# Three raw weight slices and four squared tiles in the last block, and the experts' first loads on the slices' queue

## The chip, the core and the metric

The kernel runs on one core of one Trainium2 chip. The metric is the time of one execution on the device, in microseconds (us). A core has a tensor engine (PE; its weight loads are shown as PEld), a vector engine (DVE), a scalar engine (ACT), GpSimd (POOL) and a sync engine (SP). Every engine works through its own instructions in order. DMA transfers are issued as instructions of an engine (here SP, ACT and POOL) and are carried by the core's 16 DMA engines. Data lies in SBUF (128 partitions); matmuls write to PSUM.

## The reference

Three layers follow one another. Attention with a soft cap over 4 batches of 12 heads, 448 tokens each, gives `x` of 1792 x 768. A feed-forward layer takes `h = x @ w_in` (768 x 2048), `r = max(h, 0)`, `g = s * r*r + b`, `g @ w_out`. A mixture of 8 experts with 4 slots each follows: a softmax over the tokens gathers 32 slot inputs, each expert applies `w1` (768 x 1024), a rectifier and `w2` (1024 x 768), and a softmax over the slots spreads the result over the tokens:

```python
logits = x @ phi
slot_input = softmax(logits, over tokens).T @ x
for e in range(8):
    slot_out[e] = max(slot_input[e] @ w1[e], 0) @ w2[e]
return softmax(logits, over slots) @ slot_out
```

The weights come in as 64-bit numbers in `w_in` and `w_out` and as 32-bit numbers in `w1` and `w2`; the result is 1792 x 768 in 32 bits.

## The kernel before, in words

**Blocks.** The work goes batch by batch. `block(bi)` runs the feed-forward layer of batch `bi`, while the attention of batch `bi+1` is woven in between its steps. Block 3 is the last and has no attention beside it. After it comes `tail()`, the experts.

**One slice of a block (`hidden`, 16 per block, numbered `i` through all blocks).** `w_need(i+2)` (L358) asks for a raw slice `wr` of `w_in` (384 KB), which an earlier part has converted and stored in the DRAM scratch `wsc`. `w_split(i+1)` makes from each half of a raw slice a rounded part on ACT (the CAST, L370) and the remainder on DVE (L371); the two form one `ws` tile. 18 matmuls (L386) use the two `ws` tiles of slice `i`, 9 each. ACT then writes the rectified sum into an `r2` tile (L391) and squares it in place (L392).

**After a group of four slices (`post`).** The four `r2` tiles give the logits `L` (L415, 4 matmuls) and are turned by 4 transposes each (L401), which ACT copies to `g0` and `g1` (L403). After the fourth group, `chain` works out the softmax of the block: `lt`, `ln`, `et`, the product `pt` with `g` (L473) and `ct`. In block 3 this chain stands alone at the end, behind the last matmul of the layer. For block 2 it runs inside block 3.

**Buffers.** `turns(tag, i, kept, more, last, ...)` draws a tile from a pool `kp` that lives until the end of block 3 (`kept` buffers) or from a pool `tp` that is closed before block 3 (`more` buffers). From slice `last` on, only kept buffers are used. So `wr` has 2 + 1 buffers in the blocks 0 to 2 and 2 in block 3; `r2` has 5 + 4, and 5 in block 3; `ws` has 2 half-slice tiles in block 3. A load into a `wr` buffer waits until DVE has done the split that read it last. The order of every engine's instructions is set by the scheduler of the language when the program is built.

**The experts' weights (`prefetch`).** 27 tiles `wt` of 2 MB are loaded in halves of 1 MB (L521): three tiles of `w_out`, twelve of `w1`, twelve of `w2`. Seven slots are free as soon as block 2 ends; they are filled in block 3 with 14 halves, issued on ACT's queue, each placed behind the Square of a slice. Slots 7 and 8 lie where block 3 keeps its `x`, `wr`, `ws` and `r2`; slots 9 and 10 are `g0` and `g1`. Further tiles take the slots in turn. All 40 halves from there on are issued on SP's queue.

Of the kernel before, what the change touches and what calls it, by code (L numbers as in the profile page):

```python
# [7 lines left out]
F32 = mybir.dt.float32  # L8
F32R = mybir.dt.float32r
# [8 lines left out]
P = 128  # L18
B, H, S, D = 4, 12, 448, 64
# [4 lines left out]
KC = DM // P  # L24
FF = 2048
FC = FF // P
# [7 lines left out]
SCALE = 0.125  # L34
EPS = 1e-9
CAP_FAST = 40.0
GP = 3
STEPS = 8
DIRECT = 0
CASTS = NP  # L40
# [14 lines left out]
class Body:  # L55
# [228 lines left out]
    def conv_units(self):  # L284


        nc, io, c = self.nc, self.io, self.c
        cur = {}

        def place(fc):  # L290
            return self.turns("wr", fc, 2, 1, 3 * FC - 1, [P, KC * P], F32)

        def keep(fc, o):
            self.wr[fc] = o
            if self.f64:
                nc.sync.dma_start(self.wsc[fc], o)

        def across(fh, half):
            if half == 0:
                self.wide = True  # L300
                cur["o", fh] = self.cv.tile([P, KC * U], F32, tag="o", bufs=1, name="o")
            return cur["o", fh][:, half * CU:(half + 1) * CU]

        def proj(fh, half):
            if half == 0:
                return
            o = cur.pop(("o", fh)).rearrange("p (a b) -> p a b", b=U)
            self.later = [lambda: down(fh, o)]
            if self.f64:
                self.later += [lambda th=th: wturn(fh, th, o) for th in range(3)]  # L310
            self.later.insert(2, lambda: fold(fh))

        def down(fh, o):
            pp = self.bank("pp")
            for kc in reversed(range(KC)):
                j = kc % 4
                nc.tensor.matmul(pp[32 * j:32 * j + 32, :U], c["phi"][:, kc, :], o[:, kc, :], start=(kc + 4 >= KC), stop=(kc < 4))
            nc.scalar.copy(c["tmp"][:, S + U * (fh % 2):S + U * (fh % 2 + 1)], pp[:, :U])
            self.wide = self.f64

        def fold(fh):
            ps = c["tmp"][:, S + U * (fh % 2):S + U * (fh % 2 + 1)]
            pf = self.bank("pf")
            for j in range(2):
                nc.tensor.matmul(pf[:, 32 * j:32 * j + 32], ps[:, j * P:(j + 1) * P], c["fold"][:, :32], start=True, stop=True)
            nc.vector.tensor_copy(c["pw"][:, 2 * fh:2 * fh + 2, :], pf[:, :2 * NS].rearrange("p (a b) -> p a b", b=NS))
            self.nx = fh + 1
            if self.nx == FF // U:
                self.bias()

        def wturn(fh, th, o):
            tw = self.bank("tw")
            for j in range(2):
                for k in range(2):
                    nc.tensor.transpose(tw[:, (2 * j + k) * P:(2 * j + k + 1) * P], o[:, 2 * th + k, j * P:(j + 1) * P], c["idn"])
            n = o[:, 2 * th:2 * th + 2, :].rearrange("p a b -> p (a b)")
            nc.scalar.copy(n, tw)
            nc.sync.dma_start(self.osc[th][:, 2 * U * fh:2 * U * (fh + 1)], n)
            self.wide = th < 2

        units = []
        for fc in range(FC):
            units.append((io["w_in"][fc], lambda fc=fc: place(fc), lambda o, fc=fc: keep(fc, o), lambda fc=fc: self.nsplit + 3 > fc))
            for fh in range(FF // U):
                if XPOS[fh] == fc:
                    units += [(io["w_outT"][fh, h], lambda fh=fh, h=h: across(fh, h), lambda o, fh=fh, h=h: proj(fh, h), lambda h=h: h or not self.wide) for h in range(2)]
        return units

    def w_need(self, i):

        if i >= B * FC:
            return
        if i < FC:
            while i not in self.wr:
                next(self.conv)
        else:
            self.wr[i] = self.turns("wr", i, 2, 1, 3 * FC - 1, [P, KC * P], F32)
            self.nc.sync.dma_start(self.wr[i], self.wsc[i % FC] if self.f64 else self.io["w_in"][i % FC])  # L358

    def w_split(self, i):  # L360
# [13 lines left out]
    def hidden(self, bi):  # L374
        nc = self.nc
        x = self.xtile(bi)
        for fc in range(FC):
            i = bi * FC + fc
            self.w_split(i + 1)
            self.w_need(i + 2)  # L380
            ws = self.ws.pop(i)
            hp = self.psh.tile([P, 512], F32, tag="h", bufs=2, name="hp")
            k = 0
            for kc in range(KC):
                for w, s in ((0, 0), (0, 1), (1, 0)):
                    nc.tensor.matmul(hp[:, :S], ws[kc // 3][:, w, kc % 3, :], x[:, s, kc, :], start=(k == 0), stop=(k == 3 * KC - 1))  # L386
                    k += 1
                if kc in (1, 3):
                    yield
            r2 = self.turns("r2", i, 5, 4, 3 * FC - 5, [P, S], F32)  # L390
            nc.scalar.activation(r2, hp[:, :S], AF.Relu)  # L391
            self.mark = nc.scalar.activation(r2, r2, AF.Square).ins  # L392
            self.r2[i] = r2
            yield
# [118 lines left out]
    def prefetch(self, upto, behind=False):  # L513

        while self.nslot < min(upto, 54):
            k, h = divmod(self.nslot, 2)
            if h == 0:
                self.wt[k] = self.slot(k)
            src = (self.osc if self.f64 else self.io["w_out"])[k] if k < 3 else self.io["w1"][k - 3] if k < 15 else self.io["w2"][k - 15]
            with self.tc.issue_after(self.mark) if behind else nullcontext():  # L520
                (self.nc.scalar if behind else self.nc.sync).dma_start(self.wt[k][:, 2048 * h:2048 * (h + 1)],  # L521
                                                                       src[:, 2048 * h:2048 * (h + 1)])
            self.nslot += 1

    def run(self):
# [184 lines left out]
def tile_kernel(ctx: ExitStack, tc: tile.TileContext, io):  # L710
    nc = tc.nc
# [3 lines left out]
    def t(name, shape, dt=F32):  # L715
        c[name] = cp.tile(shape, dt, name="c_" + name)
        return c[name]
# [26 lines left out]
    nc.gpsimd.dma_start(c["hot"], io["hot"])  # L744
    for n in ("s", "b"):
        nc.gpsimd.dma_start(t(n, [P, 1]), io[n + "_"].partition_broadcast(P))
    nc.gpsimd.dma_start(t("selB", [P, GP, P], F32R), io["selB"].bitcast(F32R))
    nc.gpsimd.dma_start(c["phi"], io["phi"])
    t("pbrow", [P, NS])
    t("pb", [P, 1])  # L750
# [15 lines left out]
def layouts(inputs):  # L766
    import numpy as np
    cc = np.ascontiguousarray
    q, k, v = inputs["q"], inputs["k"], inputs["v"]
    a = {}  # L770
# [29 lines left out]
    for k in range(2):  # L800
        hot[:, k, k::2] = 1
    a["hot"] = hot
    selb = np.zeros((P, GP, P), np.float32)
    for j in range(GP):
        for i in range(2):
            k = 2 * j + i
            selb[32 * (k % 4) + k // 4, j, 64 * i:64 * i + 64] = 1
    a["selB"] = selb
    return a


# [14 lines left out]
```

## Time and profile before

| what | value |
|---|---|
| three runs | 693.52, 688.12, 691.66 us |
| median | 691.66 us |
| the profiled execution's own time | 690.2 us |
| its span, from the first to the last instruction | 688.3 us |
| PE busy | 621.2 us (90% of the span) |
| DMA, mean over the span | 199 GB/s |

The profile is of one execution, so what is read from it is set against that execution's 690.2 us. Its times are counted from the start of the span. Busy shares say little by themselves, since stages with different limits follow one another; they are read stage by stage, and in each stage the wait that ends last.

### The profile page before, as it was taken

To read this page: it belongs to the slowest core of one execution; us is meant where nothing else is said; L and a number is where in the kernel's file an instruction comes from. 1 tells how busy PE (TensorE), PEld (TensorE's weight loads), DVE (VectorE), ACT (ScalarE), POOL (GpSimd) and SP (SyncE) were. 2 spreads that over 40 slices of the span, in tenths; PEclk is the share of its full clock that TensorE was granted. 3 is DMA by queue.
4 is the path that set the end of the run, shared out by engine and by line. 5 is a ranking of instruction groups with operands and counts; after the bars stand their busy time and mean duration, and the time that the engine had idled before them with its cause. 6 is when DMAs were issued, how large, how long until landed. Compare 5 with 4: busy or idle time off the path is not lost.

```text
span 688.3 us, 10613 instructions
## 1 busy us (share of the span) xinstructions
PE 621.2 (90%) x4222; PEld 396.5 (58%) x4222; DVE 386.2 (56%) x574; ACT 413.7 (60%) x688; POOL 4.6 (1%) x12
## 2 busy tenths in 40 slices
PE   3968999999999999999999999999998987987662
PEld 2323566655566566566666666667877862445552
DVE  5999998998785674744546566455331223111211
ACT  4959788977886877578767777775543551010101
POOL 2000000000000000000000000000000000000000
PEclk9979999999999999999999999999999996999997
DMA  7534468677585633122222222102867848999997
GB/s 238 192 96 143 151 239 294 219 257 265 179 283 183 211 104 119 43 94 87 65 82 86 73 88 78 50 24 62 323 206 282 307 152 359 414 418 418 418 407 237
DMA packets 45642, 136.77 MB, mean 199 GB/s; under 512 B 4352, under 2 KB 23184, under 8 KB 38672
## 3 DMA queue, kind: packets, MB, share of 16 engines
q1 hardware_dynamic: 43136, 120.60, 49.4%
q10 hardware_dynamic: 2016, 14.68, 6.0%
q8 instruction: 35, 0.57, 0.4%
q0 software_dynamic: 432, 0.72, 0.3%
q14 instruction: 23, 0.19, 0.1%
HBM read 117.90 MB, written 18.09 MB: 198 GB/s over the span
## 4 chain that ended last, share of the span: by engine, by line
PE 54%; DMA 21%; DVE 12%; ACT 7%; issue 2%; SPq 0%; ACTq 0%; DVEq 0%
PE hp L386 25%; DMA wt<-in_w_dram 10%; PE U L173 8%; PE sc L113 6%; PE tp L401 4%; DMA wr<-wsc 3%; DMA raw<-in_w_outT_dram 3%; PE pt L473 2%; PE Sm L170 2%; DMA raw<-in_w_in_dram 2%; DVE es L158 2%; DVE rec L177 2%; DMA out_dram<-wt 2%; PE L L415 2%; ACT e L149 1%
## 5 line engine op out<-in xcount | busy, mean ns | idle before, releaser
L386 PE MATMUL hp<-x,ws 128*128 128x448 f32 x1152 | 279.7, 382 | 2.3 <-ACT ws L370 2.2
L386 PEld LDWEIGHTS hp<-x,ws 128*128 128x128 f32 x1152 | 204.9, 189 | 57.0 <-issue 38.6
L371 DVE TENSOR_TENSOR ws<-wr,ws 128x384 fp32r<-128x384 f32 x128 | 70.2, 555 | 102.9 <-ACT ws L370 100.0
L116 ACT ACTIVATE e<-sc,c_tsc 112x896 f32<-112x896 f32 x96 | 96.2, 1010 | 22.4 <-PE sc L113 22.0
L173 PE MATMUL U<-e,v 112*64 112x448 f32 x384 | 88.5, 553 | 11.3 <-DVE u L179 7.0
L370 ACT CAST ws<-wr 128x384 fp32r<-128x384 f32 x128 | 65.0, 514 | 46.8 <-PE hp L386 38.4
L149 ACT ACTIVATE e<-e,c_acap 112x1792 f32<-112x1792 f32 x48 | 86.3, 1797 | 0.4
L177 DVE RECIPROCAL rec<-Sm 128x448 f32<-128x448 f32 x24 | 71.0, 2958 | 16.3 <-PE Sm L170 15.2
L173 PEld LDWEIGHTS U<-e,v 112*64 112x64 f32 x384 | 29.5, 139 | 58.1 <-issue 48.0
L158 DVE TENSOR_TENSOR es<-es,e 112x896 f32<-112x896 f32 x48 | 52.3, 1089 | 18.5 <-ACT e L149 18.2
L113 PE MATMUL sc<-qh,kh 64*112 64x448 f32 x192 | 46.1, 463 | 9.3 <-DVE kh L74 6.2
L403 ACT COPY g<-tp 112x256 f32<-112x256 f32 x128 | 41.8, 379 | 14.1 <-PE tp L401 14.0
L391 ACT ACTIVATE r<-hp 128x448 f32<-128x448 f32 x64 | 34.9, 545 | 25.6 <-PE hp L386 25.4
L113 PEld LDWEIGHTS sc<-qh,kh 64*112 64x112 f32 x192 | 17.8, 177 | 45.1 <-issue 20.9
L401 PE MATMUL tp<-c_cst,r 128*112 128x128 f32 x256 | 40.1, 277 | 2.0 <-ACT r L392 1.6
L113 PE MATMUL sc<-qh,kl 64*112 64x448 f32 x192 | 39.3, 384 | 0.4 <-DVE kl L75 0.4
L113 PE MATMUL sc<-ql,kh 64*112 64x448 f32 x192 | 39.6, 384 | 0.0
L695 ACT COPY wt<-op 128x512 f32<-128x512 f32 x12 | 7.0, 585 | 53.8 <-PE op L690 53.8
L392 ACT ACTIVATE r<-r 128x448 f32<-128x448 f32 x64 | 37.4, 585 | 0.2
L401 PEld LDWEIGHTS tp<-c_cst,r 128*112 128x112 f32 x256 | 30.0, 134 | 11.8 <-ACT r L392 2.7
L170 PE MATMUL Sm<-es,c_ones 113*64 113x448 f32 x96 | 27.0, 581 | 1.4 <-DVE es L158 1.4
L674 PE MATMUL so_ps<-wt,xt 128*32 128x128 f32 x384 | 13.9, 276 | 13.0 <-DMA wt<-in_w_dram 13.0
(140 smaller groups left out, 580.2 us busy)
## 6 DMA issues: line engine op xcount, KB each, us to landing
wt<-in_w_dram SPq DMA_DIRECT2D x40, 1024.0 KB, 19.9
wr<-wsc SPq DMA_DIRECT2D x48, 384.0 KB, 3.1
raw<-in_w_in_dram SPq DMA_DIRECT2D x16, 768.0 KB, 4.5
raw<-in_w_outT_dram SPq DMA_DIRECT2D x16, 768.0 KB, 5.7
wt<-in_w_dram ACTq DMA_DIRECT2D x8, 1024.0 KB, 6.7
wsc<-wr SPq DMA_DIRECT2D x16, 384.0 KB, 3.3
osc<-o SPq DMA_DIRECT2D x24, 256.0 KB, 3.4
wt<-osc ACTq DMA_DIRECT2D x6, 1024.0 KB, 6.4
```

What stands on the lines that cost most here:

```text
L113: nc.tensor.matmul(sc[:, i, :S], k[r, c * CP:(c + 1) * CP], q[r, :], start=(j == 0), stop=(j == 2))
L116: nc.scalar.activation(self.e[p][-1][:, :, c % 2, :], sc[:, :, :S], AF.Tanh, scale=self.c["tsc"][:CP])
L149: self.nc.scalar.activation(e, e, AF.Exp, scale=self.c["acap"][:CP])
L158: nc.vector.tensor_add(es, es, e[:, :, k, :])
L170: nc.tensor.matmul(Sm[64 * i:64 * i + 64, :S], c["ones"][:CP + 1, :64], self.es[:CP + 1, i, :], start=(p >= DIRECT), stop=True)
L173: nc.tensor.matmul(U[64 * i:64 * i + 64, :S], v[:, i, k * D:(k + 1) * D], self.chunk(2 * p + i, k), start=(k == 0), stop=(k == NCH - 1))
L177: nc.vector.reciprocal(rec, Sm[:, :S])
L370: self.nc.scalar.copy(hi, u)
L371: self.nc.vector.tensor_sub(lo, u, hi.bitcast(F32))
L386: nc.tensor.matmul(hp[:, :S], ws[kc // 3][:, w, kc % 3, :], x[:, s, kc, :], start=(k == 0), stop=(k == 3 * KC - 1))
L401: self.nc.tensor.transpose(tp[:CP, q * P:(q + 1) * P], r2[:, q * CP:(q + 1) * CP], self.c["idn"])
L403: self.nc.scalar.copy(self.g[q][:CP, :, fc * P:(fc + 1) * P], tp[:CP, 2 * q * P:2 * (q + 1) * P].rearrange("p (a b) -> p a b", b=P))
```

## The change: what it does

The pools in block 3 hold three `wr` and four `r2` buffers in place of two and five. Over the blocks 0 to 2 both have as many as before (3 and 9). A third of the tile `selB` goes, and with it its load from DRAM (the tail writes the tile before it reads it). The 14 halves of block 3 are issued by SP.

```diff
@@ conv_units and w_need, twice
-            return self.turns("wr", fc, 2, 1, 3 * FC - 1, [P, KC * P], F32)
+            return self.turns("wr", fc, 3, 0, 3 * FC - 1, [P, KC * P], F32)
@@ hidden
-            r2 = self.turns("r2", i, 5, 4, 3 * FC - 5, [P, S], F32)
+            r2 = self.turns("r2", i, 4, 5, 3 * FC - 4, [P, S], F32)
@@ prefetch
             with self.tc.issue_after(self.mark) if behind else nullcontext():
-                (self.nc.scalar if behind else self.nc.sync).dma_start(self.wt[k][:, 2048 * h:2048 * (h + 1)],
-                                                                       src[:, 2048 * h:2048 * (h + 1)])
+                self.nc.sync.dma_start(self.wt[k][:, 2048 * h:2048 * (h + 1)], src[:, 2048 * h:2048 * (h + 1)])
@@ tile_kernel
-    nc.gpsimd.dma_start(t("selB", [P, GP, P], F32R), io["selB"].bitcast(F32R))
+    t("selB", [P, 2, P], F32R)
```

`GP` was 3. Lines of the changed kernel stand one lower up to the loads of the experts (L357 is L358 of before, L369 is L370, L520 is L521).

On SP, in block 3, before: only the loads of raw slices (`wsc_96` is the first slice of the block). In brackets stands what an instruction waits for; DVE is the split that frees the buffer, DMAHW an earlier transfer.

```order
L358 DMA wr<-wsc_96 128x768 [waits DMAHW7_49,DMAHW1_49,DVE_49]
L358 DMA wr<-wsc_97 128x768 [waits DMAHW0_49,DVE_49]
L358 DMA wr<-wsc_98 128x768 [waits DMAHW3_49,DMAHW1_49,DVE_49]
L358 DMA wr<-wsc_99 128x768 [waits DMAHW2_49,DVE_49]
L358 DMA wr<-wsc_100 128x768 [waits DMAHW3_49,DVE_49]
L358 DMA wr<-wsc_101 128x768 [waits DMAHW6_49,DVE_49]
```

On SP at the same place, with the change (`wsc_97` is the third slice of the block here; the names count one lower):

```order
L357 DMA wr<-wsc_97 128x768 [waits DMAHW3_49,DMAHW0_49,DVE_49]
L520 DMA wt<-osc_111 128x2048 [waits PE_49]
L520 DMA wt<-osc_111 128x2048
L357 DMA wr<-wsc_98 128x768 [waits DMAHW1_49,DVE_49]
L520 DMA wt<-osc_112 128x2048
L357 DMA wr<-wsc_99 128x768 [waits DMAHW2_49,DVE_49]
L520 DMA wt<-osc_112 128x2048
L357 DMA wr<-wsc_100 128x768 [waits DMAHW3_49,DVE_49]
L520 DMA wt<-osc_113 128x2048 [waits PE_49]
L357 DMA wr<-wsc_101 128x768 [waits DMAHW6_49,DMAHW4_49,DVE_49]
```

The halves now stand between the slices' loads, mostly one to one, and two in a row at three places: here, before `wsc_103` and before `wsc_108`. None of them waits for ACT, though the source still places them behind a Square.

On ACT, in the middle of block 3, before: two of the halves, with the CASTs of the next slices behind them.

```order
L370 CAST ws<-wr 128x384 [waits DMAHW4_49,DVE_49,PE_49]
L403 COPY g_4520<-tp 112x2x128
L521 DMA wt<-in_w_dram 128x2048 [waits DMAHW7_49]
L370 CAST ws<-wr 128x384 [waits DVE_49,PE_49]
L403 COPY g_4519<-tp 112x2x128
L403 COPY g_4520<-tp 112x2x128
L391 ACTIVATE r_4598<-hp 128x448
L370 CAST ws<-wr 128x384 [waits DMAHW6_49,DVE_49,PE_49]
L392 ACTIVATE r_4598<-r_4598 128x448 [waits Activation_49]
L521 DMA wt<-in_w_dram 128x2048 [waits DMAHW1_49]
```

On ACT at the same slices, with the change:

```order
L369 CAST ws<-wr 128x384 [waits DMAHW4_49,DVE_49,PE_49]
L402 COPY g_4518<-tp 112x2x128 [waits PE_49]
L402 COPY g_4519<-tp 112x2x128
L369 CAST ws<-wr 128x384 [waits DVE_49,PE_49]
L390 ACTIVATE r_4597<-hp 128x448
L391 ACTIVATE r_4597<-r_4597 128x448 [waits Activation_49]
L369 CAST ws<-wr 128x384 [waits DMAHW6_49,DVE_49,PE_49]
```

The halves are gone from ACT, and the Square stands ahead of the next slice's CAST, where it stood behind it.

On PE, inside block 3, the chain of block 2 (`et`, then the product `pt`), before:

```order
L386 MATMUL hp<-x_3396,ws 128x448 x18
L461 MATMUL et_ps<-c_cst,c_tmp 112x32 x4
L473 MATMUL pt<-g_3555,c_tmp 32x512 x8
L473 MATMUL pt<-g_3556,c_tmp 32x512 x8
L493 MATMUL ct_ps<-c_cst,c_tmp 128x112 x4
```

With the change:

```order
L385 MATMUL hp<-x_3395,ws 128x448 x9
L460 MATMUL et_ps<-c_cst,c_tmp 112x32 x4
L385 MATMUL hp<-x_3395,ws 128x448 x5
L472 MATMUL pt<-g_3554,c_tmp 32x512 x8
L472 MATMUL pt<-g_3555,c_tmp 32x512 x8
L385 MATMUL hp<-x_3395,ws 128x448 x10
L492 MATMUL ct_ps<-c_cst,c_tmp 128x112 x4
```

Matmuls of the layer now stand between `et` and `pt`. The blocks 0 to 2 and the tail keep their order on PE.

## Rows read from the trace of the kernel before

**Rows 1.** Windows by stage: block 3, its closing chain, the tail's loads, the end.

```profile
core 0: us, PE busy (x) PEld busy (x) DVE busy (x) ACT busy (x) POOL busy (x), PEclk, DMA share, GB/s
479.70:561.90 82.20, 79.20 (x441) 63.86 (x439) 21.50 (x50) 41.65 (x105) 0.00 (x0) 0.98 0.69 246
561.90:587.50 25.60, 18.29 (x142) 7.81 (x146) 6.94 (x26) 4.73 (x12) 0.54 (x1) 0.73 0.89 351
587.50:659.00 71.50, 55.88 (x886) 34.72 (x874) 11.98 (x25) 6.02 (x10) 0.00 (x0) 0.98 1.01 418
659.00:688.30 29.30, 12.74 (x238) 11.11 (x238) 5.31 (x12) 3.51 (x6) 0.00 (x0) 0.83 0.86 306
```

**Rows 2.** Chain of waits, tail: start us, us, what held the chain.

```profile
570.52 6.38 PE pt L473 x32
...
587.54 10.75 DMA wt<-in_w_dram
...
638.48 20.50 DMA wt<-in_w_dram
```

**Rows 3.** Timeline of SP's issues, around block 3 and in the tail.

```profile
476.09 0.32 SPq L358 DMA_DIRECT2D wr<-wsc  x1
...
548.47 0.32 SPq L358 DMA_DIRECT2D wr<-wsc  x1
561.90 0.33 SPq L521 DMA_DIRECT2D wt<-in_w_dram  x1
...
621.09 0.33 SPq L521 DMA_DIRECT2D wt<-in_w_dram  x1
...
623.53 0.33 SPq L521 DMA_DIRECT2D wt<-in_w_dram  x1
```

**Rows 4.** Chain of waits inside block 3, from 511 us on.

```profile
511.56 1.81 issue
...
513.43 0.52 ACT ws L370
...
514.56 8.26 DMA wr<-wsc
...
522.91 0.52 ACT ws L370
...
548.47 6.90 DMA wr<-wsc
```

**Rows 5.** Timeline of PE in block 3, idle time and releaser in brackets.

```profile
498.67 3.64 PE L473 MATMUL pt<-g,c_tmp 112*32 112x512 f32 x32 [0.38 <-DVE c_tmp L463]
...
519.17 2.07 PE L386 MATMUL hp<-x,ws 128*128 128x448 f32 x9
523.48 3.03 PE L386 MATMUL hp<-x,ws 128*128 128x448 f32 x9 [2.23 <-ACT ws L370]
...
556.51 0.65 PE L401 MATMUL tp<-c_cst,r 128*112 128x128 f32 x4 [0.32 <-ACT r L392]
```

**Rows 6.** Window around that stall; the columns are those of rows 1.

```profile
520.00:530.00 10.00, 7.77 (x35) 5.54 (x34) 1.68 (x3) 2.82 (x6) 0.00 (x0) 0.83 0.77 279
```

**Rows 7.** Timeline of ACT: the CAST before that stall.

```profile
522.91 0.51 ACT L370 CAST ws<-wr 128x384 fp32r<-128x384 f32 x1 [4.77 <-DMA wr<-wsc]
```

**Rows 8.** The raw slices' loads by their line: issues, and time to landing.

```profile
L358 SPq DMA_DIRECT2D wr<-wsc x48: 319/326/499, 195.7 to 548.5; - x48
...
DMA to landing us min/median/max: 2.8/3.1/8.3
```

**Rows 9.** The halves issued on ACT from w1: ns min/median/max of the issue.

```profile
L521 ACTq DMA_DIRECT2D wt<-in_w_dram x8: 334/335/2546, 510.8 to 546.9; - x8
```

**Rows 10.** The start: selB's load among the DMA issues (KB, us).

```profile
c_selB<-in_selB_dram POOLq DMA_DIRECT2D x1, 192.0 KB, 5.8
```

**Rows 11.** Chain of waits at the start.

```profile
5.59 7.62 DMA raw<-in_w_in_dram
```

**Rows 12.** Window of that transfer; the columns are those of rows 1.

```profile
4.00:14.00 10.00, 5.38 (x24) 3.11 (x24) 6.07 (x15) 2.92 (x4) 0.57 (x2) 1.00 0.98 316
```

More of the change, by code (lines that the diff above doesn't have):

```diff
@@ L36 @@
 CAP_FAST = 40.0
-GP = 3
 STEPS = 8
@@ L356, in w_need @@
         else:
-            self.wr[i] = self.turns("wr", i, 2, 1, 3 * FC - 1, [P, KC * P], F32)
+            self.wr[i] = self.turns("wr", i, 3, 0, 3 * FC - 1, [P, KC * P], F32)
             self.nc.sync.dma_start(self.wr[i], self.wsc[i % FC] if self.f64 else self.io["w_in"][i % FC])
@@ L802, in layouts @@
     a["hot"] = hot
[L803 to L808, printed above, removed]
     return a
```

## The prediction

> **What bounds the kernel now.** I read the windows by stage first. In block 3, from 479.7 to 561.9 us, PE is busy 79.2 of 82.2 us, while the DMA engines move 246 GB/s [rows 1]. In the tail, from 587.5 to 659 us, it is the other way round: DMA share 1.01 at 418 GB/s, with PE waiting for weights [rows 1]. So block 3 is bound by PE and the tail by transfers. The chain of waits confirms the second: from 587.54 to 658.98 us it consists of loads of the experts' weights, the last piece of it 20.5 us long [rows 2].
>
> Next, what joins the two stages. SP issues the first of the last 40 halves at 561.90 us [rows 3], when the last matmul of the layer has freed its `x`; the `g` slots come free only with `pt`, which runs from 570.52 for 6.38 us [rows 2]. Both hang on the end of block 3. A microsecond won there therefore starts the saturated transfers a microsecond earlier, and the tail passes it on to the end. A microsecond won on transfers inside block 3 is worth nothing unless PE waits for one.
>
> Does PE wait for one? The timeline of PE has one large hole: 9 matmuls begin at 523.48 after 2.23 us of idling, released by the CAST [rows 5]. That CAST had itself waited 4.77 us for the load of its raw slice [rows 7], issued at 514.56 and 8.26 us on the way [rows 4], where the median of all these loads is 3.1 us [rows 8]. The window from 520 to 530 us shows a granted clock of 0.83, against 0.98 for the block as a whole [rows 6, 1]; the 9 matmuls that took 2.07 us just before the hole took 3.03 after it [rows 5]. So the hole is paid twice, once as idling and once at the lower of the clock's two levels (1.2 against 2.4 GHz).
>
> **The change part by part.**
>
> *Third raw slice.* A load waits until the split that read its buffer is done. With three buffers that is the split of one slice earlier. The 15 loads from 476.09 to 548.47 us stand 72.38 / 14 = 5.17 us apart [rows 3], so a load can go out about 5.2 us earlier. The late slice landed at 514.56 + 8.26 = 522.82 us and cost PE 2.23; it was needed at 520.59, which is 6.0 us after its issue. With three buffers it may take 6.0 + 5.2 = 11.2 us. The longest landing seen is 8.3 us [rows 8]. I therefore take away the whole 2.23 us, and the clock's loss behind it, which I read as 10 us x (1 - 0.83) = **1.7 us** [rows 6]. The bounds of the clock's part are nothing, if the clock falls for another reason, and 1.9 us, if it explains all of the slower pieces behind the hole as well.
>
> *Halves on SP instead of ACT.* ACT loses 14 issues of about 0.33 us, one of them 2.5 us long [rows 9]. That long one stands in the chain ahead of the hole: 1.81 us of issue, then the CAST, then the split, and only then the late slice's load [rows 4]. It is part of how the hole came about and is not counted again. ACT is busy 41.65 of 82.2 us [rows 1], and PE has no other hole that an issue on ACT explains, so the other issues count nothing: the cover is PE's own work, and if it were gone each would cost its 0.33 us.
>
> On SP each slice's load now has halves ahead of it in the same queue, two in a row at three places of the new order. SP itself is not held: of the halves only a few wait for anything, the rest ride behind the slice ahead. In the tail, with the engines saturated, the queue takes a half every 623.53 - 621.09 = 2.44 us [rows 3]. Two halves ahead make 4.9 us, and the slice's own 3.1 us makes 8.0 us, still 3.2 us inside the 11.2. So I put the cost at nothing. Its upper bound is the first rival.
>
> A slice and a half issued by two engines stand in two queues before, and in one after. The Trainium skill (DMA: Bandwidth & Descriptors, section Queues, rings and completion order) says that each DMA engine goes round between the queue rows that have work, a packet at a time, and takes the descriptors of one ring in order. By that rule the slice was protected on its own queue: it would have had every second packet, and the hole would not have been there; the gain would then be only the 1.0 us of the small terms below, and the time 689.2. The trace does not agree: with halves on the other queue the slice took 8.26 and, later, 6.90 us instead of 3.1 [rows 4, 8]. The measurement decides, and the sum keeps the hole.
>
> *The order of PE and ACT.* Two small waits go. Before `pt` of block 2, PE waited 0.38 us for DVE [rows 5]; five matmuls of the layer now stand there, about five ninths of 2.07 us, which covers it. The 0.32 us before 556.51 came from a Square [rows 5] that stood on ACT behind a CAST which waited for a slice until 548.47 + 6.90 = 555.37 us [rows 4]; with the slice in time it goes. Together **0.7 us**. The rest of PE's new order has the same instructions.
>
> *Four squared tiles.* A new `r2` is written after the matmuls of its slice, and the transposes that free the tile of four slices before stand ahead of those matmuls on PE. Nothing waits. If that cover failed, the price would be one group of transposes, 0.65 us [rows 5], a few times.
>
> *selB.* One load of 192 KB less [rows 10], issued into a stretch in which the chain waits 7.62 us for a raw weight [rows 11] while the engines move 316 GB/s at a share of 0.98 [rows 12]. 0.197 MB / 316 GB/s = 0.6 us is the most it can give; nothing is the least, since it travels in another queue. I take **0.3 us**. The issue that POOL saves has no waiter.
>
> **Sum.** 2.23 + 1.7 + 0.7 + 0.3 = 4.9 us. Against the profiled execution's 690.2 us this gives 685.3. The median of the three runs is 691.66, 1.5 us above that execution, which would put it at 686.8. I take 686 us, a gain of 0.8% on the median. About 1% (6.9 us, so 684.7 or 698.6) is what a measurement of this kernel can tell from no change.
>
> **Rivals.**
>
> *The joint queue makes slices late (slower).* Mechanism: SP issues halves without waiting for a Square, so more than two stand ahead of a slice. It decides once a slice takes longer than 11.2 us from issue to landing; 4 halves ahead (9.8 + 3.1 = 12.9 us) would do it. The places are the three doubled halves. Price: each a hole like the one now seen, 2.23 + 1.7 = 3.9 us, three of them 11.8. Time: 690.2 - 4.9 + 11.8 = 697.1 us. For it: 8.26 us has been seen even with two queues [rows 4]. Against: per slice a half and a slice need some 2.44 + 0.9 us of the engines in 5.17 us, so that the queue drains. Chance 8%. The Trainium skill's sentence on rings taken in order (DMA: Bandwidth & Descriptors, Queues, rings and completion order) is what would make it so.
>
> *The hole is mostly this execution's.* The three runs differ by 5.4 us; in others the late load may not be late, or the clock may fall anyhow. Then only 0.7 + 0.3 us remain: 689.2 us, or 690.7 set against the median. For it: of 48 such loads only a few were late enough to hold ACT; against it: two slices late in one block [rows 4] look like a habit. Chance 18%. The Trainium skill's rule on queue rows served in turn (same page and section) would have it so too.
>
> *More comes than the hole.* The closing chain runs at 0.73 of the clock [rows 1], and `pt` takes 6.38 us [rows 2] where the same product of block 2 took 3.64 [rows 5]. Shifted by 5 us and ahead of a PE that did not stall, it may fall into a stretch at the full clock. That frees the `g` slots up to 2.7 us earlier: 685.3 - 2.7 = 682.6 us. Against: PE idles in this chain just as before. Chance 14%.
>
> **How the numbers follow.** The forecast keeps 60%, with 683.5 to 688.5 us as its own range. The range 682 to 691 us takes in the second and third rivals and leaves out the first and some of the spread at each end. Faster by over 1% means below 684.7: a quarter of the forecast's 60% and two thirds of the last rival, 0.25. Slower by over 1%: half of the first rival and a little for what I have not seen, 0.06. The rest, 0.69, lies within 1%.
>
> **What would show it.** In the profile after: no idle of PE in block 3 that a CAST or a raw slice ends; a granted clock of 1.00 through block 3; the raw slices landing later than 3.1 us in the median, up to 8 us, and still no wait of ACT for them; the first half of the last 40 issued at about 557 us instead of 561.9; from there the same tail at 418 GB/s, each mark some 5 us earlier. I am wrong if ACT waits for raw slices again, if block 3 ends earlier and the tail does not, or if the block ends where it did.

## The result, and the profile after

The changed kernel took 682.66 us (median of 4 runs, 681.42 to 683.84), the kernel before 690.13 us in runs beside it (4 runs, 688.12 to 693.52). The ratio is 0.9886, with a 95% interval from 0.985 to 0.9922: 7.5 us, 1.1% faster. The forecast was 686 us in a range from 682 to 691, so that the median lies 0.7 us inside its lower end. Two later timings of the same kernel, among the experiments, gave 0.9923 and 0.9888 with medians of 684.76 and 684.79 us; the three intervals overlap.

The profiled execution after took 683.84 us, with a span of 682.0 us (before: 688.3 us). To see where the 6.3 us between the two spans came from, I cut both at the same events: the first `U` matmul, the first `L` matmul of block 2's last group, the last `hp` matmul of block 3, and SP's issue of the last half.

| stretch | before, us | after, us | change |
|---|---|---|---|
| start to the first `U` matmul | 15.86 | 14.57 | -1.29 |
| from there to block 3 | 464.51 | 467.56 | +3.05 |
| block 3 | 81.50 | 75.77 | **-5.73** |
| end of block 3 to SP's issue of the last half | 87.15 | 87.12 | -0.03 |
| that issue to the end | 39.28 | 36.98 | **-2.30** |

The first two rows are read as scatter: their instructions stand in the same order in both kernels. In the profiles below, the second stretch lasts from 464.4 to 469.8 us with three slice buffers (six profiles) and from 464.2 to 467.7 us with two (eight profiles). The two kinds overlap, but a cost of a microsecond or so of the third buffer in that stretch is not excluded. What the change moved for certain stands in the two bold rows. The windows after, by the cuts of [rows 1] shifted with the block's end, and a last one over block 3 by the events of the table:

```profile
core 0: us, PE busy (x) PEld busy (x) DVE busy (x) ACT busy (x) POOL busy (x), PEclk, DMA share, GB/s
481.50:557.90 76.40, 76.40 (x441) 62.81 (x439) 21.88 (x50) 44.27 (x105) 0.00 (x0) 1.00 0.66 253
557.90:583.50 25.60, 18.26 (x139) 7.70 (x142) 6.95 (x26) 4.51 (x12) 0.54 (x1) 0.73 0.89 351
583.50:655.00 71.50, 55.89 (x890) 34.62 (x878) 11.98 (x25) 6.25 (x10) 0.00 (x0) 0.97 1.01 418
655.00:682.00 27.00, 13.63 (x238) 12.09 (x238) 5.31 (x12) 3.51 (x6) 0.00 (x0) 0.82 0.93 331
482.13:557.90 75.77, 75.77 (x438) 62.51 (x437) 21.86 (x49) 43.80 (x104) 0.00 (x0) 1.00 0.66 252
```

In block 3 PE is now busy for the whole window, at a granted clock of 1.00. The closing chain and the saturated tail read as before: clock 0.73, then 418 GB/s at a DMA share of 1.01. Block 3 by the same events before, for comparison:

```profile
480.37:561.87 81.50, 78.52 (x438) 63.52 (x437) 21.45 (x49) 41.13 (x104) 0.00 (x0) 0.98 0.70 248
```

The 5.73 us are thus 2.98 us of idling and 2.75 us of PE's busy time, for the same 438 matmuls.

On PE's timeline after, none of block 3's waits of [rows 5] is left:

```profile
497.88 3.64 PE L472 MATMUL pt<-g,c_tmp 112*32 112x512 f32 x32
...
512.84 10.59 PE L385 MATMUL hp<-x,ws 128*128 128x448 f32 x51
...
555.83 2.07 PE L385 MATMUL hp<-x,ws 128*128 128x448 f32 x9
```

`pt` no longer waits for DVE, and 51 `hp` matmuls in a row run through the stretch in which the 2.23 us hole was. The raw slices' loads, which [rows 8] shows over the whole program, tell more when the view is cut to block 3, from 470 to 565 us. Their issues and their time to landing there, before:

```profile
L358 SPq DMA_DIRECT2D wr<-wsc x15: 319/319/320, 476.1 to 548.5; - x15
...
DMA to landing us min/median/max: 2.8/5.8/8.3
```

And after:

```profile
L357 SPq DMA_DIRECT2D wr<-wsc x14: 319/320/327, 477.9 to 540.2; - x14
...
DMA to landing us min/median/max: 2.8/3.4/6.2
```

The median falls from 5.8 to 3.4 us, where the forecast had expected later landings, up to 8 us. Over all 48 loads the median is 3.1 us in both, and hides this.

How the two kinds of transfer now follow each other is seen on SP's timeline after (start, duration, line, operation):

```profile
510.48 0.33 SPq L357 DMA_DIRECT2D wr<-wsc  x1
510.85 0.43 SPq L520 DMA_DIRECT2D wt<-in_w_dram  x1
515.47 0.33 SPq L357 DMA_DIRECT2D wr<-wsc  x1
515.84 0.43 SPq L520 DMA_DIRECT2D wt<-in_w_dram  x1
...
557.94 0.33 SPq L520 DMA_DIRECT2D wt<-in_w_dram  x1
```

A half goes out 0.37 us behind a slice, and the next slice only about 4.6 us after that half, because SP waits in between for a split to free a buffer. Before, ACT issued two halves close around one slice: one at 510.79, an issue 2.55 us long, and the next at 514.97, with the slice of [rows 4] at 514.56 between them:

```profile
510.79 2.55 ACTq L521 DMA_DIRECT2D wt<-in_w_dram  x1
514.97 0.34 ACTq L521 DMA_DIRECT2D wt<-in_w_dram  x1
```

What that slice met on its way stands in the packets of the DMA view. `q10` carries what ACT issues, and has nothing in the profile after; `q1` carries what SP issues. The columns are packets, MB and the share of the 16 engines' time. First before's window from 515.5 to 517 us, a microsecond behind the slice's issue, then the one from 518.5 to 521 us:

```profile
q10 hardware_dynamic: 78, 0.63, 100.1%
```

```profile
q10 hardware_dynamic: 103, 0.82, 82.9%
q1 hardware_dynamic: 58, 0.16, 15.9%
```

At first only the half issued ahead moved. Then the half issued behind the slice took 82.9% of the engines' time, and the slices' queue 15.9%, though the slice was still on its way until 522.82. So on a queue of its own the slice had to wait for most of both halves. On one queue with them, the half that goes out 0.37 us behind a slice no longer makes it late.

The first of the last 40 halves leaves at 557.94 instead of 561.90 us [rows 3]. The chain after keeps its steps of [rows 2], `pt` among them at 6.56 us:

```profile
566.56 6.56 PE pt L472 x32
...
645.02 19.96 DMA wt<-in_w_dram
```

### The profile page after: what moved, and what is told of

Same layout as the page of the kernel before. It is cut to its first block, busy times and chain, and to the rows that moved or that the text cites. A ratio compares the mean times of both kernels' runs of the same rounds, so it can differ in the third digit from the quotient of the medians.

```text
span 682.0 us, 10606 instructions
## 1 busy us (share of the span) xinstructions
PE 620.0 (91%) x4222; PEld 396.8 (58%) x4222; DVE 386.8 (57%) x574; ACT 416.8 (61%) x688; POOL 4.1 (1%) x11
## 4 chain that ended last, share of the span: by engine, by line
PE 60%; DMA 17%; DVE 12%; ACT 6%; issue 2%; SPq 1%; DVEq 0%; ACTq 0%
PE hp L385 28%; DMA wt<-in_w_dram 11%; PE U L172 9%; PE sc L112 6%; PE tp L400 4%; DMA raw<-in_w_outT_dram 3%; DMA raw<-in_w_in_dram 3%; PE Sm L169 3%; PE pt L472 3%; DVE es L157 2%; DVE rec L176 2%; PE L L414 2%; PE si_ps L631 1%; ACT e L148 1%; PE tw L334 1%
## 5 line engine op out<-in xcount | busy, mean ns | idle before, releaser
L370 DVE TENSOR_TENSOR ws<-wr,ws 128x384 fp32r<-128x384 f32 x128 | 70.4, 555 | 99.7 <-ACT ws L369 96.7
L369 ACT CAST ws<-wr 128x384 fp32r<-128x384 f32 x128 | 65.2, 514 | 37.3 <-PE hp L385 37.1
L176 DVE RECIPROCAL rec<-Sm 128x448 f32<-128x448 f32 x24 | 70.9, 2956 | 16.8 <-PE Sm L169 15.8
L112 PE MATMUL sc<-qh,kh 64*112 64x448 f32 x192 | 46.4, 465 | 10.8 <-DVE kh L73 6.2
```

Source lines behind the costliest of these rows:

```text
L112: nc.tensor.matmul(sc[:, i, :S], k[r, c * CP:(c + 1) * CP], q[r, :], start=(j == 0), stop=(j == 2))
L176: nc.vector.reciprocal(rec, Sm[:, :S])
L369: self.nc.scalar.copy(hi, u)
L370: self.nc.vector.tensor_sub(lo, u, hi.bitcast(F32))
```

## The experiments

Two theories stood at the start. **T1**, the forecast's: the third raw buffer removes the hole, and the halves' move to SP costs and gives nothing. **T2**, its rival: the gain comes from the halves' queue. In the expectations below they are called A and B; C is the load of selB. Then come the size of the deadline, and what lies behind the gain at the end. "Block 3" and "last half to end" are the stretches of the table above, from each run's profile.

| run | time against before | median, us | block 3 | slices' landing there, median / longest | last half to end | SP's second store of `out`, issue |
|---|---|---|---|---|---|---|
| before | 1 | 690.13 | 81.50 | 5.8 / 8.3 | 39.28 | 5.22 |
| after | 0.9886 (0.985 to 0.9922) | 682.66 | 75.77 | 3.4 / 6.2 | 36.98 | 0.39 |
| e1, queue alone | 0.9924 (0.9897 to 0.9951) | 685.04 | 75.90 | 3.4 / 4.4 | 37.97 | 0.39 |
| e2, buffers alone | 0.9933 (0.9907 to 0.9959) | 685.78 | 77.25 | 5.8 / 9.3 | 39.22 | 3.02 |
| e3, selB alone | 1.0027 (0.9999 to 1.0056) | 693.52 | 81.60 | 5.9 / 8.6 | 40.42 | 5.13 |
| e4, the change again | 0.9923 (0.9891 to 0.9955) | 684.76 | 75.76 | 3.6 / 6.1 | 36.97 | 1.48 |
| e5, two slices, ACT issues 1/16 | 0.9865 (0.9813 to 0.9916) | 682.61 | 75.81 | 3.8 / 5.5 | 36.95 | 0.39 |
| e6, fours, two slices | 1.0035 (1.0001 to 1.0069) | 694.20 | 83.95 | 3.6 / 9.9 | 36.55 | 0.76 |
| e7, fours, three slices | 0.9933 (0.9898 to 0.9968) | 687.68 | 78.40 | 4.0 / 10.8 | 37.24 | 0.39 |
| e8, sevens, three slices | 1.003 (0.9997 to 1.0063) | 693.92 | 84.43 | 3.3 / 18.0 | 36.88 | 1.47 |
| e9, before again | one run | 688.37 | 81.10 | 6.0 / 8.6 | 39.26 | 5.16 |
| e10, w1's halves on ACT | 0.9905 (0.9871 to 0.9939) | 685.77 | 79.01 | 4.6 / 7.8 | 37.11 | 1.48 |
| e11, the change again | 0.9888 (0.9851 to 0.9926) | 684.79 | 75.77 | 3.6 / 6.0 | 37.02 | 0.39 |
| e12, as e5 | 0.9886 (0.9844 to 0.9929) | 683.38 | 76.43 | 4.1 / 6.2 | 36.90 | 1.47 |

**e1: the queue alone.** Two slices, five squared tiles and selB as before:

```diff
-                (self.nc.scalar if behind else self.nc.sync).dma_start(self.wt[k][:, 2048 * h:2048 * (h + 1)],
+                self.nc.sync.dma_start(self.wt[k][:, 2048 * h:2048 * (h + 1)],
```

> Only the 14 halves of block 3 move from ACT's queue to SP's; two raw slices, five squared tiles and selB's load stay. Theory A (the third slice buffer takes the hole away; the queue is neutral): with two buffers a slice may still take only about 6.0 us to land, and behind one or two halves it takes 5.5 to 8 us, so ACT waits for slices as before or more often; 690 to 694 us, block 3 (from the L matmuls of block 2's last group to the last matmul of the layer) 81 to 85 us where before took 81.5. Theory B (the halves on ACT made the hole, by their issue time and as a second queue): the hole goes, block 3 about 76 us, 684 to 686 us. Theory C (selB's load at the start): no change from this edit, 690.

The window of block 3, and the slices behind which the halves ride:

```profile
480.61:556.51 75.90, 75.89 (x438) 62.46 (x437) 21.86 (x49) 43.82 (x104) 0.00 (x0) 1.00 0.68 256
```

```profile
508.95 0.33 SPq L358 DMA_DIRECT2D wr<-wsc  x1
509.32 0.43 SPq L521 DMA_DIRECT2D wt<-in_w_dram  x1
513.94 0.33 SPq L358 DMA_DIRECT2D wr<-wsc  x1
514.31 0.43 SPq L521 DMA_DIRECT2D wt<-in_w_dram  x1
```

The hole is gone with two buffers. SP's spacing is that of the changed kernel: the half ahead of a slice is 4.6 us old when the slice goes out. The slices land after 3.4 us in the median and 4.4 at most, inside even the forecast's limit of 6.0 us for two buffers. So the queue alone is enough.

**e2: the buffers alone.** The halves stay on ACT; selB is two thirds as large, to make room:

```diff
-GP = 3
+GP = 2
...
-            self.wr[i] = self.turns("wr", i, 2, 1, 3 * FC - 1, [P, KC * P], F32)
+            self.wr[i] = self.turns("wr", i, 3, 0, 3 * FC - 1, [P, KC * P], F32)
...
-            r2 = self.turns("r2", i, 5, 4, 3 * FC - 5, [P, S], F32)
+            r2 = self.turns("r2", i, 4, 5, 3 * FC - 4, [P, S], F32)
```

> Three raw slices and four squared tiles in block 3, the halves still issued by ACT; selB is two thirds of its size, so that it fits, and that part is still loaded. Theory A: no wait of ACT for a slice in block 3, PE without the hole and at a granted clock of 1.00, block 3 about 76 to 77 us, 684 to 686 us. Theory B: ACT's issues still delay the CASTs and the slices' loads; block 3 80 us or more, 688 to 690 us. Theory C: 689.5 (a third of selB's load less).

First PE's timeline and ACT's, then the window of block 3, then the loads of the slices in it:

```profile
503.43 3.64 PE L473 MATMUL pt<-g,c_tmp 112*32 112x512 f32 x32 [0.38 <-DVE c_tmp L463]
...
530.12 0.96 PE L415 MATMUL L<-r,c_hh 128*32 128x448 f32 x8 [0.59 <-ACT r L392]
```

```profile
529.08 0.51 ACT L370 CAST ws<-wr 128x384 fp32r<-128x384 f32 x1 [2.04 <-DMA wr<-wsc]
```

```profile
485.14:562.39 77.25, 76.23 (x438) 62.37 (x437) 21.43 (x49) 41.40 (x104) 0.00 (x0) 1.00 0.73 257
```

```profile
DMA to landing us min/median/max: 3.0/5.8/9.3
```

The slices are as late as before, two of them 9.3 us, and PE still had no hole behind a CAST: the third buffer takes the hole away, as the forecast said. The granted clock is 1.00, so the hole's idling and clock are won with the buffers alone as well. But the forecast expected no wait of ACT for a slice, and there is one of 2.04 us. What is left against the changed kernel is 77.25 - 75.77 = 1.48 us: the 0.38 us before `pt`, 0.59 us before an `L` matmul that waited for a Square on ACT, which stood behind a CAST that the late slice (issued at 519.66) had held for 2.04 us, and 0.46 us of PE's busy time (76.23 against 75.77). So a CAST that waits on ACT cost PE something here through the Square behind it, without being late for its own matmuls.

**e3: selB's load alone.** The tile stays, its load goes:

```diff
-    nc.gpsimd.dma_start(t("selB", [P, GP, P], F32R), io["selB"].bitcast(F32R))
+    t("selB", [P, GP, P], F32R)
```

> Only selB's load of 192 KB at the start is left out. Theory C: the first raw slice lands 0.6 to 1.3 us earlier, U of the first pair starts about 14.6 us where before had 15.86, and the time is 689 us. Theories A and B: the start may move by as much, but what it gives is lost in the attention's own waits before block 3; 690 us.

1.0027, with an interval from 0.9999: no gain. The first raw weight's wait at the start, 7.62 us in [rows 11], was 6.20 us after, but 7.75 in e11, the same kernel. So it moves by itself.

**e4 and e11: the change again,** for its scatter, e4 timed beside e1 to e3 and e11 beside e12:

> The changed kernel once more, beside the other three. All theories: 682.7 us, within 1; block 3 75.8 us, no wait for a slice. If the tail from the last matmul of the layer to the end is again 2.3 us shorter than before's 126.4 us, the change has to do with it; if it scatters by as much from run to run, it is no part of the change.

> The changed kernel, beside the next run for a direct comparison. Block 3 75.8 us, the end of the span below 38 us behind the last half, 0.99 of before.

Block 3 repeats within 0.01 us (75.77, 75.76, 75.77); the rest of the execution does not, and the medians came out 2 us above the expected 682.7. The end is 2.3 us shorter than before's each time.

**e5 and e12: ACT keeps its issues, SP moves the data.** Two slices; of each half's 2048 columns ACT issues 128 and SP the other 1920:

```diff
-                (self.nc.scalar if behind else self.nc.sync).dma_start(self.wt[k][:, 2048 * h:2048 * (h + 1)],
-                                                                       src[:, 2048 * h:2048 * (h + 1)])
+                if behind:
+                    self.nc.scalar.dma_start(self.wt[k][:, 2048 * h:2048 * h + 128], src[:, 2048 * h:2048 * h + 128])
+                    self.nc.sync.dma_start(self.wt[k][:, 2048 * h + 128:2048 * (h + 1)], src[:, 2048 * h + 128:2048 * (h + 1)])
```

> As before (two raw slices, five squared tiles, selB loaded), but each of the 14 halves is cut: ACT issues the first 128 of its 2048 columns, at the place where it issued the half, and SP issues the other 1920 behind the slices. ACT thus keeps all 14 issues, SP's queue carries the data. Theory of the issue time (the halves on ACT held back its CASTs, and so the slices' loads): the hole stays, block 3 80 us or more, 688 to 691 us. Theory of the one queue (a half that stands behind a slice in SP's order can't delay that slice): no hole, block 3 about 76 to 77 us, 684 to 687 us.

> The kernel with a sixteenth of every half issued by ACT and the rest by SP, two raw slices, again, with more rounds. If its first ratio of 0.9865 is more than scatter it comes out below the changed kernel again, by 2 to 3 us; since its block 3 took 75.8 us as well, I expect no difference from the changed kernel that stands clear of the interval: 0.988 to 0.993.

```profile
481.27:557.08 75.81, 75.81 (x438) 62.43 (x437) 21.88 (x49) 43.64 (x104) 0.00 (x0) 1.00 0.69 257
```

The window of e5's block 3 has no idle time, with 14 issues on ACT, and the slices land after 3.8 us in the median (e12: 4.1, its longest of 6.2 us with 0.27 us of idling of PE). So what the queue gives is not ACT's short issues saved, but where the bulk of a half's bytes stands. With ratios of 0.9865 and 0.9886 these two are as fast as the change itself (0.9886); the intervals don't part them from it. e5's 682.61 us lies below the 684 to 687 that were expected.

**e6 and e7: four halves ahead of a slice.** The halves are gathered in bunches of four, and SP keeps the written order; e6 has two slices (with e1's edit), e7 is the changed kernel with the same bunches:

```diff
-                self.block(3, None)
+                with tc.manual_schedule(engines={nc.sync.engine}):
+                    self.block(3, None)
...
-                if last and k % 3 == 0:
-                    self.prefetch(min(14, 4 * grp + k // 3 + 2), True)
+                if last and k == 0 and True:
+                    self.prefetch(min(14, 4 * grp + 4), True)
```

> Halves on SP, two raw slices (as in the run with the queue alone), but SP keeps the written order and gets the halves in bunches of four at the start of each group of slices. A slice that is issued some 5 us behind a bunch finds 9.8 - 5 us of it still ahead, and takes about 8 us. Theory of the deadline (6.0 us with two buffers, 11.2 with three): about 2 us late in each group, holes of 2 to 4 us with the slow clock behind them, block 3 80 to 88 us, 688 to 696 us. Rival (the queue move alone is enough, whatever the order on SP): 76 us, 685 us.

> The changed kernel with the same bunches of four. Theory of the deadline: 8 us stays within 11.2, no hole, block 3 about 76 us, 683 to 686 us. Rival (a slice behind a bunch makes PE wait with three buffers as well): holes as in the run with two slices.

PE's timeline and the loads of the slices in block 3, in e6:

```profile
523.69 5.93 PE L386 MATMUL hp<-x,ws 128*128 128x448 f32 x27 [1.15 <-ACT ws L370]
...
544.20 7.25 PE L386 MATMUL hp<-x,ws 128*128 128x448 f32 x27 [1.82 <-ACT ws L370]
```

```profile
DMA to landing us min/median/max: 3.0/3.6/9.9
```

The same in e7:

```profile
537.80 6.01 PE L385 MATMUL hp<-x,ws 128*128 128x448 f32 x27 [0.44 <-ACT ws L369]
```

```profile
DMA to landing us min/median/max: 2.9/4.0/10.8
```

Bunches do make slices late: three land after 9.4, 9.4 and 9.9 us in e6, and three after 9.1 to 10.8 us in e7. With two buffers PE has holes of 1.15 and 1.82 us, with three one of 0.44 us. ACT's timeline shows how much of that is a slice's doing. First the CASTs that end the two holes of e6, then the one of e7:

```profile
523.12 0.94 ACT L370 CAST ws<-wr 128x384 fp32r<-128x384 f32 x2
543.64 0.92 ACT L370 CAST ws<-wr 128x384 fp32r<-128x384 f32 x2 [0.57 <-DMA wr<-wsc]
```

```profile
537.24 0.93 ACT L369 CAST ws<-wr 128x384 fp32r<-128x384 f32 x2
```

Only the second waited for a slice, for 0.57 us. In e6 both stand behind the copies of a group to `g`; in e7 the CAST stands behind a rectifier and a copy, and its slice had landed 3 us earlier. So ACT's order, which the scheduler had also made anew, has a part in these holes, and e7 has no wait for a slice at all. Its block of 78.40 us missed the 76 that were expected: 0.82 us of the excess are idling, 1.81 are busy time of PE, and the cause of the latter is open. **e8** goes further, with two bunches of seven in the changed kernel, again in the written order:

```diff
-                if last and k % 3 == 0:
-                    self.prefetch(min(14, 4 * grp + k // 3 + 2), True)
+                if last and k == 0 and grp % 2 == 0:
+                    self.prefetch(min(14, 7 + 7 * (grp // 2)), True)
```

> The changed kernel with the halves in two bunches of seven, at the start of the first and the third group. 7 x 2.45 = 17.1 us, less some 5 us until the next slice is issued, plus 3.1: about 15 us. Theory of the deadline: some 4 us late at each of the two bunches, so two holes with the slow clock behind them; block 3 83 to 88 us, 690 to 695 us. Rival (later slices make good what one loses): no hole, 76 us.

```profile
504.01 5.92 PE L385 MATMUL hp<-x,ws 128*128 128x448 f32 x27 [1.37 <-ACT ws L369]
...
544.39 7.09 PE L385 MATMUL hp<-x,ws 128*128 128x448 f32 x27 [4.12 <-ACT ws L369]
```

```profile
DMA to landing us min/median/max: 2.9/3.3/18.0
```

```profile
543.83 0.93 ACT L369 CAST ws<-wr 128x384 fp32r<-128x384 f32 x2 [2.87 <-DMA wr<-wsc]
```

The holes are back, and block 3 takes 84.43 us. The hole of 4.12 us belongs to a slice that landed after 17.9 us and held ACT for 2.87. The landing of 18.0 us, early in the block, made ACT wait for nothing, and the hole of 1.37 us again has a CAST behind copies at its end. e6 and e8 thus took the times and blocks that the theory of the deadline gave, by holes that are its doing only in part. In these three kernels the scheduler also put PE's instructions a little differently, so their block times are not compared to the last tenth, nor their limits.

**e9: before again,** for a second trace of the hole:

> The kernel before once more, for a second trace of it. All theories: the hole in block 3 again, 81 to 82 us for the block. Open is the end: from SP's issue of the last half to the end of the span the traces with halves on ACT took 39.2 to 40.4 us and those without 36.5 to 38.0, and SP's issue of the second store took 3.0 to 5.2 us in the first kind. If that is a property of the kernel it comes again; if the end scatters by itself, it comes out below 38.

```profile
523.25 2.28 PE L386 MATMUL hp<-x,ws 128*128 128x448 f32 x9 [2.70 <-ACT ws L370]
...
546.15 0.67 PE L386 MATMUL hp<-x,ws 128*128 128x448 f32 x2 [0.77 <-ACT ws L370]
```

```profile
479.60:560.70 81.10, 77.16 (x438) 62.20 (x437) 21.46 (x49) 41.06 (x104) 0.00 (x0) 1.00 0.70 250
```

The hole comes at the same place, now 2.70 us with 0.77 later, and the clock stays at 1.00. So the hole is a habit of the kernel; whether it is paid a second time by the clock changes from one execution to the next. With the clock at 1.00 PE is busy for 77.16 us, against 78.52 in the first trace: the slow clock cost 1.4 us there. That still leaves 1.4 us above the 75.77 of the changed kernel.

**e10: only the six halves of w_out on SP,** the eight of w1 on ACT, two slices:

```diff
-                (self.nc.scalar if behind else self.nc.sync).dma_start(self.wt[k][:, 2048 * h:2048 * (h + 1)],
+                (self.nc.scalar if behind and k >= 3 else self.nc.sync).dma_start(self.wt[k][:, 2048 * h:2048 * (h + 1)],
```

> Two raw slices, as before; the first six halves go to SP, the eight from w1 stay on ACT. Theory of the one queue: the second half of block 3 keeps its two queues and its hole, block 3 79 to 82 us, 688 to 691 us. On the long issue on ACT (2.5 to 2.9 us at the seventh half in three traces): if it belongs to the seventh issue of that queue, it moves to the last but one; if to the first half out of w1, it stays with that; if it belongs to neither, it is gone.

A slice, the half that ACT issues 0.70 us behind it, the CAST and PE, from the timelines:

```profile
518.09 0.32 SPq L358 DMA_DIRECT2D wr<-wsc  x1
...
518.79 0.33 ACTq L521 DMA_DIRECT2D wt<-in_w_dram  x1
...
525.94 0.51 ACT L370 CAST ws<-wr 128x384 fp32r<-128x384 f32 x1 [3.95 <-DMA wr<-wsc]
...
526.99 0.96 PE L415 MATMUL L<-r,c_hh 128*32 128x448 f32 x8 [2.50 <-ACT r L392]
```

With the halves on the other queue the late slice is back, and 2.50 us of idling with it, though no issue of a half on ACT was longer than 0.42 us in this run. So the long issue of [rows 9] is not needed for the hole. Block 3 took 79.01 us, as the theory of the one queue expected; the time of 685.77 us is 2 us below what was expected, and the end behind the last half is 2.2 us shorter than before's.

## Why the prediction was right, and where it was short

The hole was read rightly and is gone, and the time is in the range. The forecast's own span of 683.5 to 688.5 us was missed by 0.8 us with the first median and met with the two later ones. Part of the agreement is luck: the forecast put the whole gain down to the buffers, and the queue, which it put at nothing, takes the hole away by itself as well.

**What bounds the two stages** held. A microsecond won in block 3 came out at the end: from the block's end to the last half's issue it was 87.15 us before and 87.12 after.

**The third slice buffer** held, and with two buffers so did its arithmetic. The forecast put the slice's time limit at 6.0 us with two buffers and 11.2 with three. With two buffers, longest landings of 8.3, 8.6 and 8.6 us (before, e3, e9) came with holes of 2.23, 2.84 and 2.70, which puts the limit at 5.7 to 6.0; 4.4 and 5.5 us (e1, e5) came with none, 6.2 (e12) with 0.27. The limit is not every slice's: beside block 2's chain, 8.5 us in e3 cost PE nothing. The 11.2 us with three buffers are less well shown. 9.3 us (e2) made no `hp` matmul wait, but already cost 0.59 us through a Square; 10.8 (e7) made ACT wait for nothing; the 17.9 us of e8 with its hole of 4.12 would give 13.8, with the order changed. Alone the buffers were worth 81.50 - 77.25 = 4.25 us in block 3, where hole, clock and Square had been put at 2.23 + 1.7 + 0.32, which is 4.25 as well. That fit is luck: of the 4.25 measured, 1.96 us were idling and 2.29 busy time, and e9's block of 81.10 us had more idling and no slow clock.

**The clock's 1.7 us** was about right, and the term beside it was missing. In the block as a whole the forecast took away 2.93 us of idling and 1.7 for the clock. Measured are 2.98 and 2.75 us. By e9 the clock has 1.4 of the latter (78.52 - 77.16). The other 1.4 (77.16 - 75.77) is busy time at the full clock, which the forecast put at nothing ("The rest of PE's new order has the same instructions"). What makes the same matmuls shorter is open.

**"Halves on SP instead of ACT"**, whose cost and gain the forecast put at nothing, is the step that was mis-sized. Beside the third buffer the move gave another 1.48 us in block 3, of which the forecast had only the 0.38 before `pt`. In the kernel with two buffers it removes the hole by itself and gives 81.50 - 75.90 = 5.60 us (e1), so the two parts overlap and their gains must not be added. The step went wrong where it priced the joint queue: two halves ahead at 2.44 us each were to make a slice's load 8.0 us long. That price is of the saturated tail, where halves are issued back to back. In block 3 SP waits for a split between one slice and the next, so that a half is mostly 4 to 5 us old before the next slice goes out. Behind halves 2.9 and 3.3 us old, slices took 5.3 and 6.2 us, the two longest after. And the slices came sooner on the joint queue, not later: 3.4 to 3.6 us in the median with the change, 5.8 to 6.0 in the four profiles with all halves on ACT. The forecast saw that the halves "ride behind the slice ahead", and asked what this costs the next slice, not what it spares the same one. e5 and e10 show that it is the place of the bytes that counts and not ACT's issue. How the engines share themselves among two queues the packets of before show: beside a half, the slices' queue got 15.9% of their time; e9 has 16.8% from 518 to 520.5 us. By the Trainium skill (DMA: Bandwidth & Descriptors, Queues, rings and completion order) a slice on a row of its own takes turns with the halves' row, packet by packet. The trace has packets of both queues in the same stretch, but the turns are not equal shares: a half's packets are 8 KB and a slice's 3 KB (0.82 MB in 103 packets and 0.16 MB in 58), and there were almost twice as many of the former. That is what the forecast's "every second packet" left out. It kept the hole in its sum because the two late loads of before spoke against the rule, and that choice was right.

**"The same tail at 418 GB/s, each mark some 5 us earlier"** was short at its end. The last half's issue comes 4.0 us earlier (645.02 against 649.02, as block 3 began 1.8 us later in this execution), and the end 6.3 us. Between them lie 39.2 to 40.4 us in the four profiles with all 14 halves on ACT (before, e9, e2, e3), and 36.5 to 38.0 in the ten others. The same four have a long issue of SP's second store of `out`, here before and then after:

```profile
663.20 5.22 SPq L699 DMA_DIRECT2D out_dram<-wt  x1
```

```profile
660.49 0.39 SPq L697 DMA_DIRECT2D out_dram<-wt  x1
```

Before, the chain of waits passed through that store, 12.44 us from 663.20 on, and after it doesn't. But in e9 the chain runs through the last weights instead, with the same long issue beside it, so that the issue is a companion of the 2.3 us and not shown to be its cause. Nor is a long issue of a store peculiar to these four: SP's fourth store takes 3.55 us after and 3.62 in e10. This part stays open. The forecast could not have it from a row that it had read.

**selB, 0.3 us:** not borne out (e3). **Four squared tiles, nothing:** in block 3 ACT waits once in e2, 0.57 us, for an `L` matmul to free its tile, and never after; PE paid nothing for it.

**The rivals.** The joint queue does make slices late, where four or seven halves are gathered (e6, e8), but the change's longest landing in block 3 is 6.2 us, far inside 11.2. That the hole was this execution's is out: the three other profiles with halves of w1 on ACT and two slices have holes (2.84 us in e3, 2.70 in e9, 2.50 in e10). The closing chain at full clock did not come: `pt` took 6.56 us after, 6.38 before. That the first median is the 682.6 us of this rival is chance: it was reached by another way, in block 3 and at the end.

Taken together: 5.73 us in block 3 and 2.30 at the end make 8.0 us; the start and the middle, -1.29 + 3.05, hid 1.8 of it in this pair of profiles. The forecast's sum was 4.9. The 5.73 can't be split between the parts in one way: the buffers alone give 4.25, the queue alone 5.60.

## What to carry to other kernels

When a transfer with a deadline is late, work out its limit from its issue and the wait that it caused, and how much one more buffer adds; here the 6.0 us for two buffers were borne out within 0.3 us. Look also at what stands behind the late instruction on its engine, since that waits with it. When transfers are moved to another queue, ask what they spare as well as what they delay: one in-order queue whose engine waits for a buffer between issues spaced the bulk transfers out for nothing. A queue of its own did not protect a small transfer: count the packets of each queue while both are at work before relying on turns. Two edits that each remove the same wait give their gain once, so try each alone before adding them.

## What the runs showed of the hardware

- A load of 384 KB on a queue of its own, beside 1 MB loads on another, landed after 5.8 to 6.0 us in the median of block 3 and 9.3 at most; on one queue with them, one or two bulk loads behind a load, after 3.4 to 4.1 us and 6.2 at most.
- One issue on ACT took 2.55 us before (2.5 to 2.9 in all four profiles with the 14 halves on ACT), where its others take 0.33, and SP's second store 3.0 to 5.2 us, against 0.4 to 1.5 in the ten other profiles. With the first six halves on SP and eight on ACT (e10) neither appears, though another store takes 3.62 us there. Why is open.
- While a 1 MB load on ACT's queue and 384 KB loads on SP's were both at work, the first had 82.9% of the engines' time and the others 15.9% (before, 518.5 to 521 us), with packets of 8 and 3 KB.
- The same hole of PE cost the clock in one execution (0.83 in the window of [rows 6]; 78.52 us of busy time in the block) and not in another (1.00 through e9's block 3; 77.16 us).
